# Induced attention in front of two MLPs: narrowing steps placed apart, one softmax for the first chunk, its second block spread early, and second-MLP products held back at exponentials

## The chip, the cores and the metric

The kernel runs on one core of one Trainium2 chip. The metric is the device time of one execution in microseconds, the median of several runs. The core's engines are TensorE (PE in the rows, its weight loads PEld), VectorE (DVE), ScalarE (ACT), GpSimd (POOL) and SyncE (SP), which issues most of the DMAs. Each engine works through its own queue in program order and waits on semaphores for the others.

## What is computed

```python
def mab(q, kv):                       # attention with one head
    s = scale * (q @ kv.transpose(0, 2, 1))
    s = s - s.max(-1, keepdims=True)
    a = np.exp(s)
    a /= a.sum(-1, keepdims=True) + 1e-09
    return a @ kv

h = mab(I, x)            # 32 inducing points over x: 12480 tokens of 128
y = mab(x, h)            # every token over the 32 points
t = y @ w_in;  y = (t * np.cos(t)) @ w_out        # first MLP, 128 -> 2048 -> 128
t = y @ w_in2; y = (t / (1 + np.exp(-t))) @ w_out2  # second MLP, the same sizes
```

The four weight matrices arrive as 64-bit floats.

## The kernel before

The kernel has a prologue, a branch on a flag, and a main loop that is written out in full.

**Heads.** The prologue walks over x in eight heads of 5 to 16 tiles of 128 tokens (`heads`, L70). For each, TensorE transposes the tiles in two halves (`transposes`), ScalarE and VectorE copy them out (`untile`: the first half by ScalarE, the second by VectorE for two groups of 32 rows and then by ScalarE for the other two), TensorE makes the scores against the inducing points, VectorE takes the maximum (`scores`), a running bias is built (`row_max`, `bias`), ScalarE takes the exponential (`exps`), VectorE transposes it (`turn`), and TensorE adds to the attention sum (`induced`, `rescale`). The loop from L565 interleaves these for heads i, i-1 and i-2, and the order of the calls is the order in each engine's queue.

**Narrowing.** A weight matrix is cut into four pieces of 128 x 512; 16 pieces stand in `order` (the first MLP's in and out, then the second's). `fetch` loads a raw 64-bit piece over SP's queue into one of RAW buffers. `narrow_words` makes two parts on ScalarE (body and tail, L137 and L138), `narrow_sign` masks the sign on VectorE (L143), `narrow_join` shifts and joins on VectorE (L148) and adds on POOL (L158), and the next piece is fetched. `begin` runs the ScalarE half and returns the rest as a function to be called later. Pieces 0 to 3 go beside heads 3 to 6, with sign and join behind `turn`; piece 4 in the prologue's end; pieces 5 to 15 in steps 0 to 16 of the main loop, ScalarE's and VectorE's halves in the same step. `split` makes the pair of a rounded value (ScalarE, L172) and the rest (POOL, L173) of a piece.

**Second attention.** Tokens are taken in seven chunks: 8 tiles, five times 16, and 10. For a chunk, `weigh_scores` (TensorE), take, centre, exp, norm, turn and split make the weights: into `s2`, then into `at` and `ahi`, tiles which all chunks share. The chunk's blocks of up to 512 columns are then spread by `spread`: four DMAs of each group of 32 rows, at most 64 KB each, two from `ahi` and two from `at`, into one of two halves of `stk`. Block 0 and block 1 are the first chunk's first and second four tiles in all four groups, so these take 16 DMAs each, or for block 0 a matrix product with `pick` in the prologue; chunk k > 0 has four blocks, one for each group, with four DMAs. In the prologue the first chunk's two halves are two softmaxes (`soft[0]`, `soft[1]`); the second is finished in main steps 1 to 3, and its spread stands at step 4.

**Main loop.** There are 26 blocks of 8 units (a unit is 256 of the 2048 hidden columns), and step s of the loop at L963 runs unit s of the first MLP and unit s - 11 of the second: `mlp1_in` (2 products of TensorE, L752), `mlp2_in` (6, L859), `mlp1_act` (cosine on ScalarE, L781, product on VectorE, L784, rounded half, L790), `mlp2_act` (Silu and rounded half on ScalarE, rest on POOL), `mlp2_out` (unit s - 13), `mlp1_rest` (VectorE, L801) and `mlp1_out` (unit s - 1), the down projections by six products each (L811). In the first 12 units of the first MLP and the first 8 of the second the down projection takes one fp32 product in place of three of the faster form (L821). The hidden values of the second MLP have one PSUM buffer (`h2`), those of the first two. A chunk's take also writes to `h2`. Cosine and Silu need another activation table than the exponential, so each chunk's exponential stands between two table loads on ScalarE. The loop's calls are again the order of the queues:

```python
v = s - L2
if 0 <= v < NU:
    mlp2_in(v)
...
attend(s, True)          # a chunk's exponential
if 0 <= v < NU:
    mlp2_act(v)
```

Of the kernel before, what the change touches and what calls it, by code (L numbers as in the profile page):

```python
# [21 lines left out]
def tile_induced_attention_then_two_mlps(  # L22
# [82 lines left out]
    EARLY = 5  # L105
    PF = 4
    PC, RAW = PF * P, 3
    NP = NF // PF
    raw = persist.tile([P, RAW, PC], I64, name="raw")
    cv = ctx.enter_context(tc.tile_pool(name="cv", bufs=1, reuse_waits="tile"))  # L110
# [18 lines left out]
    parts = {}  # L129

    def narrow_words(name, j):
        words = raw[:, order.index((name, j)) % RAW, :]
        words = words.bitcast(I32).rearrange("p (n w) -> p n w", w=2)
        low, high = words[:, :, 0], words[:, :, 1]
        body = cv.tile([P, PC], F32, tag="body", name="body")
        tail = cv.tile([P, PC], I32, tag="tail", name="tail", bufs=2)
        nc.scalar.mul(body, high.bitcast(F32), 2.0**-112)  # L137
        nc.scalar.mul(tail, low.bitcast(U32), 2.0**-29)  # L138
        parts[name, j] = high, body, tail

    def narrow_sign(name, j):
        sign = cv.tile([P, PC], I32, tag="sign", name="sign")
        nc.vector.tensor_scalar(sign, parts[name, j][0], -(2**31), None, ALU.bitwise_and)  # L143
        parts[name, j] += (sign,)

    def narrow_join(name, j, dst=None):
        high, body, tail, sign = parts.pop((name, j))
        nc.vector.scalar_tensor_tensor(  # L148
            out=sign,
            in0=body.bitcast(I32),  # L150
            scalar=3,
            in1=sign,
            op0=ALU.logical_shift_left,
            op1=ALU.bitwise_or,
        )
        if dst is None:
            dst = tail.bitcast(F32)
        nc.gpsimd.tensor_tensor(dst.bitcast(I32), sign, tail, ALU.add)  # L158
        return dst
# [4 lines left out]
    def split(name, j, v, hi_on=nc.scalar.copy, lo_on=nc.gpsimd):  # L164
        pair = pair_of[name]
        if name[0] == "i":
            hi, lo = (w[:, j * PC : (j + 1) * PC] for w in pair)
        else:
            hi, lo = (
                w[:, PF * j : PF * (j + 1), :].rearrange("p f d -> p (f d)") for w in pair  # L170
            )
        hi_on(hi, v)  # L172
        lo_on.tensor_tensor(lo, v, hi.bitcast(F32), ALU.subtract)  # L173

    narrowed = {}

    def narrow(name, j):

        narrow_words(name, j)
        yield  # L180
        narrow_sign(name, j)
        if name == "in1":
            v = narrow_join(name, j, win[:, j * PC : (j + 1) * PC])
        elif name[0] == "o":
            v = whole_view(name, j)
            narrow_join(name, j, v)
        else:
            v = narrow_join(name, j)
        narrowed[name, j] = v
        fetch()  # L190

    def whole_view(name, j):
        if name in whole_of:
            return whole_of[name][:, PF * j : PF * (j + 1), :].rearrange("p f d -> p (f d)")

    def begin(k):
        step = narrow(*order[k])
        next(step)
        return lambda: next(step, None)
# [26 lines left out]
    def weigh_view(t0, nt, a=0):  # L226
# [4 lines left out]
        for name in ("at", "hi"):  # L231
            st[name] = sft[name][:, a * Q : (a + nt) * Q]
        return st
# [56 lines left out]
    def spread(b, st):  # L290
        t0 = st["span"][0]
        stack = stk[:, b % 2, :]
        for g, t, m, at, n in places(b):
            a = (t - t0) * Q
            for r in range(G):
                src = st["hi"].bitcast(F32) if r < 2 else st["at"]
# [6 lines left out]
    with ExitStack() as pro:  # L303
        pp = pro.enter_context(tc.tile_pool(name="pp", bufs=1))
        pw = pro.enter_context(tc.tile_pool(name="pw", bufs=2))
        ps_s = pro.enter_context(tc.tile_pool(name="ps_s", bufs=2, space=PSUM))
        ps_t = pro.enter_context(tc.tile_pool(name="ps_t", bufs=2, space=PSUM))
        ps_h = pro.enter_context(tc.tile_pool(name="ps_h", bufs=1, space=PSUM))
        ps_m = pro.enter_context(tc.tile_pool(name="ps_m", bufs=1, space=PSUM))
# [25 lines left out]
        for k in range(NH):  # L335
            load(k)
            if 3 <= k < 3 + RAW:
                fetch()
# [223 lines left out]
        end = NH - 1  # L562

        beside = {3: 0, 4: 1, 5: 2, 6: 3}
        for i in range(end):  # L565
            finish = None
# [5 lines left out]
            untile(i, 1)  # L572
            if i >= 2:
                induced(i - 2)
# [14 lines left out]
        untile(end, 0)  # L589
        transposes(end, 1)  # L590
# [5 lines left out]
        scores(end)  # L596
        induced(end - 2, (KT // 2, KT))
# [5 lines left out]
        finish = begin(4)  # L603
# [32 lines left out]
        nc.scalar.activation(sq[:, 0:M], misc[:C, 0:M], AF.Square)  # L636

# [34 lines left out]
        weigh_take(soft[0])  # L672
        weigh_centre(soft[0], nc.vector)
        weigh_exp(soft[0])
        weigh_take(soft[1])
        weigh_centre(soft[1], nc.gpsimd)
        project_hi(0)
        weigh_exp(soft[1])
# [353 lines left out]
```

## Time and profile before

| what | value |
|---|---|
| median of 3 runs | 1006.03 us (1004.76 to 1008.72) |
| the profiled execution | 1005.34 us |
| its span, first to last instruction | 1003.50 us |
| TensorE busy | 968.4 us, 96% |
| VectorE, ScalarE, POOL busy | 788.3, 703.3, 509.0 us |
| heads and first attention, until about | 43 us |
| first product of block 0 | 49.99 us |

A row of a timeline has its start, its length, engine, line, operation, the tiles it writes and reads, and, in brackets, how long the engine stood idle before it and what ended that. TensorE works nearly without a gap from about 120 us on; in front of that the engines take turns in waiting. The granted clock of TensorE is given as a share of full speed, 2.4 GHz; 0.50 is its other level, 1.2 GHz.

### The profile page before, as it was taken

How to read it: one execution, taken by the hardware profiler on the slowest of the kernel's cores; microseconds unless marked ns; L12 is line 12 of the kernel's file. 1: busy time of each engine (PE TensorE's matmuls, PEld its weight loads, DVE VectorE, ACT ScalarE, POOL GpSimd, SP SyncE). 2: the span in 40 equal slices, each digit the busy share in tenths (PEclk: the TensorE clock that was granted, in tenths of full speed). 3: DMA queues.
4: the chain of work that ended last, by engine and by line, in shares of the span. 5: the costliest groups of instructions: out<-in, count | busy, mean ns of one | idle time of the engine just before them, and what ended most of it. 6: DMA issues, size and time to landing. Idle time of an engine off the chain costs nothing.

```text
span 1003.5 us, 12438 instructions
## 1 busy us (share of the span) xinstructions
PE 968.4 (96%) x4667; PEld 774.1 (77%) x4667; DVE 788.3 (79%) x824; ACT 703.3 (70%) x766; POOL 509.0 (51%) x268
## 2 busy tenths in 40 slices
PE   8877999999999999999999999999999999999997
PEld 6533677788887788887788887788887788889996
DVE  4783878898888888888888888888888888867871
ACT  5666566777676777676777676777676777777774
POOL 1143354555554555555565555564545555556555
PEclk9987999999999999999999999999999999999999
DMA  9232000100100100100100100100100100000000
GB/s 339 65 115 85 22 9 14 22 11 10 22 11 11 22 11 12 21 11 11 22 11 11 21 11 11 22 11 11 22 11 11 22 11 8 18 17 11 14 8 16
DMA packets 65230, 28.22 MB, mean 28 GB/s; under 512 B 54312, under 2 KB 59784, under 8 KB 65160
## 3 DMA queue, kind: packets, MB, share of 16 engines
q1 hardware_dynamic: 64504, 27.24, 11.1%
q8 instruction: 39, 0.64, 0.3%
q14 instruction: 31, 0.25, 0.1%
q10 hardware_dynamic: 656, 0.09, 0.1%
HBM read 14.79 MB, written 6.39 MB: 21 GB/s over the span
## 4 chain that ended last, share of the span: by engine, by line
PE 87%; DVE 5%; ACT 4%; issue 2%; SPq 1%; POOL 1%; DMA 0%; DVEq 0%; ACTq 0%; POOLq 0%
PE acc L811 48%; PE h L859 26%; PE h L752 8%; PE acc L821 2%; ACT c L781 2%; PE s L421 1%; SPq L297 1%; ACT L874 1%; ACT s L874 1%; DVE sign L148 1%; DVE h L784 1%; PE pt L388 1%; DVE hi L790 1%; DVE lo L801 1%; DMA stk<-at 0%
## 5 line engine op out<-in xcount | busy, mean ns | idle before, releaser
L883 POOL TENSOR_TENSOR lo<-s,hi 128x1024 fp32r<-128x1024 f32 (+2 forms) x197 | 447.7, 2273 | 390.3 <-ACT hi L882 353.0
L811 PE MATMUL acc<-hi,wo 128*128 128x512 f32 (+2 forms) x1584 | 409.3, 380 | 0.0
L781 ACT ACTIVATE c<-h,half_pi 128x1024 f32<-128x1024 f32 (+2 forms) x208 | 221.0, 1063 | 172.3 <-PE h L752 172.3
L784 DVE TENSOR_TENSOR h<-h,c 128x1024 f32<-128x1024 f32 (+2 forms) x196 | 227.5, 1161 | 140.9 <-ACT c L781 140.6
L811 PEld LDWEIGHTS acc<-hi,wo 128*128 128x128 f32 x1584 | 288.5, 188 | 57.8 <-issue 2.2
L859 PE MATMUL h<-yhi,wi 128*128 128x512 f32 (+2 forms) x832 | 249.1, 381 | 11.7 <-ACT s L874 9.4
L874 ACT ACTIVATE s<-h 128x1024 f32<-128x1024 f32 (+2 forms) x208 | 202.4, 973 | 67.8 <-PE h L859 65.5
L811 PE MATMUL acc<-lo,wo 128*128 128x512 f32 (+2 forms) x792 | 235.4, 378 | 0.1
L790 DVE CAST hi<-h 128x1024 fp32r<-128x1024 f32 (+2 forms) x196 | 226.1, 1153 | 6.8
L801 DVE TENSOR_TENSOR lo<-h,hi 128x1024 fp32r<-128x1024 f32 (+2 forms) x196 | 225.1, 1148 | 5.9
L882 ACT CAST hi<-s 128x1024 fp32r<-128x1024 f32 (+2 forms) x197 | 196.7, 998 | 6.3
L859 PEld LDWEIGHTS h<-yhi,wi 128*128 128x128 f32 x832 | 151.8, 188 | 46.5 <-ACT s L874 14.2
L811 PEld LDWEIGHTS acc<-lo,wo 128*128 128x128 f32 x792 | 145.7, 188 | 29.5 <-POOL lo L888 0.4
L859 PE MATMUL h<-ylo,wi 128*128 128x512 f32 (+2 forms) x416 | 157.4, 378 | 0.0
L752 PE MATMUL h<-stk,hw 128*128 128x512 f32 (+2 forms) x416 | 129.3, 392 | 10.4 <-DMA stk<-at 6.4
L752 PEld LDWEIGHTS h<-stk,hw 128*128 128x128 f32 x416 | 76.8, 191 | 37.3 <-issue 15.0
L859 PEld LDWEIGHTS h<-ylo,wi 128*128 128x128 f32 x416 | 78.4, 188 | 14.6
L844 ACT CAST yhi<-acc 128x512 fp32r<-128x512 f32 (+2 forms) x26 | 14.6, 561 | 18.7 <-PE acc L811 13.7
L821 PE MATMUL acc<-c,wf 128*128 128x512 f32 x48 | 26.7, 685 | 0.9 <-DVE ylo L845 0.9
L845 DVE TENSOR_TENSOR ylo<-acc,yhi 128x512 fp32r<-128x512 f32 (+2 forms) x26 | 16.8, 648 | 8.8 <-ACT yhi L844 8.8
L906 DVE STREAM_TRANSPOSE o<-acc 128x512 f32<-128x512 f32 (+2 forms) x26 | 17.5, 673 | 7.6 <-PE acc L811 7.6
L784 DVE TENSOR_TENSOR c<-h,c 128x1024 f32<-128x1024 f32 x12 | 14.6, 1213 | 9.0 <-ACT c L781 9.0
(141 smaller groups left out, 333.2 us busy)
## 6 DMA issues: line engine op xcount, KB each, us to landing
out_dram<-o SPq DMA_DIRECT2D x80, 64.0 KB, 2.0
x_sb<-in_x_dram SPq DMA_DIRECT2D x8, 512.0 KB, 7.5
raw<-in_moe_w_in_dram SPq DMA_DIRECT2D x8, 512.0 KB, 5.1
raw<-in_moe_w_out_dram SPq DMA_DIRECT2D x8, 512.0 KB, 3.8
stk<-ahi SPq DMA_DIRECT2D x40, 64.0 KB, 2.0
stk<-at SPq DMA_DIRECT2D x40, 64.0 KB, 2.0
x_sb<-in_x_dram SPq DMA_DIRECT2D x3, 256.0 KB, 3.2
x_sb<-in_x_dram SPq DMA_DIRECT2D x2, 320.0 KB, 10.9
```

The source lines that it names most:

```text
L752: nc.tensor.matmul(ps[:, a, 0:n], lhsT=hw[f // 4][:, f % 4 * P : (f % 4 + 1) * P], rhs=stacks[b][:, 0:n], start=True, stop=True,)
L781: nc.scalar.activation(cs, h, AF.Sin, bias=half_pi, scale=1.0)
L784: nc.vector.tensor_tensor(cs if whole else h, h, cs, ALU.mult)
L790: nc.vector.tensor_copy(hi[:, :, 0:n], h)
L801: nc.vector.tensor_tensor(lo[:, :, 0:n], h, hi[:, :, 0:n].bitcast(F32), ALU.subtract)
L811: nc.tensor.matmul(acc[:, 0:n], lhsT=wt[:, 2 * j + a, :], rhs=gt[:, a, 0:n], start=(j == 0 and p == 0 and a == 0), stop=(j == NJ - 1 and p ...
L821: nc.tensor.matmul(acc[:, 0:n], lhsT=w[:, 2 * j + a, :], rhs=c[:, a, 0:n], start=(j == 0 and a == 0), stop=(j == NJ - 1 and a == 1),)
L859: nc.tensor.matmul(ps[:, a, 0:n], lhsT=wt[:, fs], rhs=yt[:, 0:n], start=(p == 0), stop=(p == 2),)
L874: nc.scalar.activation(sv, hid2.pop(u)[:, :, 0:n], AF.Silu)
L882: nc.scalar.copy(hv, sv)
L883: nc.gpsimd.tensor_tensor(lv, sv, hv.bitcast(F32), ALU.subtract)
L906: nc.vector.transpose(o.rearrange("p t d -> p (t d)")[:, 0:n], acc2.pop(b)[:, 0:n])
```

## The change

- **Narrowing in single steps.** `narrow_body`, `narrow_tail`, `narrow_sign` and `narrow_join` are called one by one; body, tail and sign become persistent tiles (two buffers of body and tail), the raw pieces get four buffers instead of three, and the first raw load stands one head earlier in SP's queue. In the heads body goes behind the copies and tail behind the exponentials of heads 2 to 5; sign and join go in front of the scores of heads 3 to 6. Piece 4 is narrowed at the last head and joined behind the projection's start; body and tail of piece 5 go where piece 4 was. In the main loop a piece's join is mostly one step behind its body and tail.
- **One softmax for the first chunk.** The two halves are weighed as one chunk of 8 tiles in the prologue; the steps 1 to 3 of `second` fall away.
- **Block 1 spread in the prologue**, right behind block 0's stack, with the 16 DMAs on SP's queue ahead of the branch; the source of its rest part is `lo0`, a tile of the prologue's pool.
- **Chunk 1's softmax** has its exponential at step 12 instead of 11, norm 13, turn 14 and split in the same step (14.5) instead of the step behind turn.
- **Held back.** In the step behind a chunk's exponential `mlp2_in` and `mlp2_act` stand at the step's end, in the one after it behind `mlp2_out`.
- **Smaller ones.** The cosine's tile has one buffer instead of two from unit 12 on; the prologue's PSUM pools are opened in another order, so the main loop's PSUM tiles take the banks of other tiles; blocks 3 to 5 are spread five steps ahead instead of eight (steps 19, 27 and 35). Chunk 2's turn and split, which write the same `at` and `ahi`, stay at steps 34 and 35, so block 5's spread comes behind them in the order of the program, and copies what chunk 2 left there.

```diff
-        beside = {3: 0, 4: 1, 5: 2, 6: 3}
         for i in range(end):
+            k = i - 2 if i < 2 + NP else None
             ...
             untile(i, 1)
+            if k is not None and k >= 0:
+                narrow_body(k)
             ...
                 exps(i - 1)
-            if i in beside:
-                finish = begin(beside[i])
+            if k is not None and k >= 0:
+                narrow_tail(k)
             if i >= 2:
                 rescale(i - 2)
+            if 0 <= i - 3 < NP:
+                narrow_sign(i - 3)
+                narrow_join(i - 3)
             scores(i)
             if i >= 1:
                 turn(i - 1)
-            if finish:
-                finish()
...
-        soft = [weigh_view(MT * b, MT, MT * b) for b in range(2)]
-        for b, st in enumerate(soft):
-            ps = ps_s.tile([P, W], F32, tag="s1", name="s2")
-            weigh_scores(st, ps[:, 0 : MT * Q])
+        first = chunk_soft[0]
+        weigh_scores(first, ps_s.tile([P, W], F32, tag="s1", name="s2")[:, 0:WF])
...
         stacks[0] = stk[:, 0, :]
+        spread(1, first | {"lo": lo0.bitcast(F32)})
...
-    narrowing = dict(zip((0, 1, 2, 3, 5, 7, 9, 11, 12, 14, 16), order[EARLY:]))
+    worded = dict(zip((0, 1, 2, 4, 6, 8, 10, 12, 14, 16), range(NP + 2, 4 * NP)))
+    joined = dict(zip((0, 1, 2, 3, 5, 7, 9, 11, 13, 15, 17), range(NP + 1, 4 * NP)))
...
-    second = {1: "norm", 2: "turn", 3: "split"}
-    third = {3: "take", 5: "centre", 11: "exp", 12: "norm", 13: "turn", 14: "split"}
+    second = {3: "take", 5: "centre", 12: "exp", 13: "norm", 14: "turn", 14.5: "split"}
...
+                bufs=2 if whole else 1,
...
+        held_back = {}
+        for k in range(1, NK):
+            for s in range(NU):
+                if chunk_step(k, s) == "exp":
+                    held_back[s + 1], held_back[s + 2] = 2, 1
...
+            place = held_back.get(s, 0)
+            into = [False] * 3
             if 0 <= v < NU:
+                into[place] = True
+            if into[0]:
                 mlp2_in(v)
             ...
             attend(s, True)
-            if 0 <= v < NU:
+            if into[0]:
                 mlp2_act(v)
             v = s - L2 - D2
             if 0 <= v < NU:
                 mlp2_out(v)
                 ...
+            v = s - L2
+            if into[1]:
+                mlp2_in(v)
+                mlp2_act(v)
             if s < NU:
                 mlp1_rest(s)
             if s >= L2:
                 out1(s)
+            if into[2]:
+                mlp2_in(v)
+                mlp2_act(v)
```

## Rows read from the trace of the kernel before

**Rows 1.** Page, busy time, share of the span and instructions by engine.

```profile
PE 968.4 (96%) x4667; PEld 774.1 (77%) x4667; DVE 788.3 (79%) x824; ACT 703.3 (70%) x766; POOL 509.0 (51%) x268
```

**Rows 2.** Windows: length, busy of PE, PEld, DVE, ACT, POOL, granted clock, DMA.

```profile
76.40:82.50 6.10, 6.07 (x9) 3.17 (x10) 1.22 (x1) 1.62 (x2) 1.52 (x2) 0.50 0.51 169
...
96.60:100.00 3.40, 3.40 (x8) 2.55 (x9) 1.90 (x2) 3.04 (x5) 1.29 (x1) 0.55 0.02 5
```

**Rows 3.** Timeline of PE, the first transposes of heads 3, 4 and 5.

```profile
15.06 1.09 PE L388 MATMUL pt<-ident,x_sb 128*128 128x128 f32 x8
...
19.52 1.09 PE L388 MATMUL pt<-ident,x_sb 128*128 128x128 f32 x8
...
24.62 1.09 PE L388 MATMUL pt<-ident,x_sb 128*128 128x128 f32 x8
```

**Rows 4.** Timeline of DVE, sign and join of piece 0, the scores' maximum.

```profile
20.96 0.42 DVE L143 TENSOR_SCALAR sign<-raw 128x512 int32<-128x512 int32 x1
21.48 0.69 DVE L148 SCALAR_TENSOR_TENSOR sign<-body,sign 128x512 int32<-128x512 int32 x1
...
24.74 0.69 DVE L431 TENSOR_REDUCE mx<-s 128x1 f32<-128x512 f32 x1 [1.45 <-PE s L421]
```

**Rows 5.** Timeline of DVE, two transposes and the projections' second halves.

```profile
11.38 0.43 DVE L504 STREAM_TRANSPOSE et<-e 128x256 f32<-128x256 f32 x1
...
43.60 0.32 DVE L239 STREAM_TRANSPOSE s<-s 128x128 f32<-128x128 f32 x1 [0.63 <-PE s L218]
...
48.51 2.72 DVE L653 SCALAR_TENSOR_TENSOR hw<-hw,s_w,hwps 128x512 fp32r<-128x512 f32 x4 [0.99 <-ACT hw L650]
```

**Rows 6.** The branch's line (last number: start), and block 0's first product.

```profile
L990 PEldq TENSOR_LOAD <-flag x1: 487/487/487, 47.6 to 47.6; - x1
...
L990 SPq TENSOR_LOAD <-flag x1: 484/484/484, 52.1 to 52.1; - x1
...
49.99 0.74 PE L752 MATMUL h<-stk,hw 128*128 128x512 f32 x2 [1.42 <-ACT stk L698]
```

**Rows 7.** Timeline of PE, main loop: waits and starts of steps.

```profile
76.43 1.19 PE L752 MATMUL h<-stk,hw 128*128 128x512 f32 x2 [5.28 <-DMA stk<-at]
...
90.40 1.03 PE L752 MATMUL h<-stk,hw 128*128 128x512 f32 x2
96.56 1.22 PE L859 MATMUL h<-yhi,wi 128*128 128x512 f32 x2 [5.13 <-ACT s L874]
...
119.04 0.70 PE L752 MATMUL h<-stk,hw 128*128 128x512 f32 x2 [1.11 <-DMA stk<-at]
...
182.58 0.62 PE L752 MATMUL h<-stk,hw 128*128 128x512 f32 x2
...
187.17 0.62 PE L752 MATMUL h<-stk,hw 128*128 128x512 f32 x2
188.68 0.73 PE L859 MATMUL h<-yhi,wi 128*128 128x512 f32 x2 [0.89 <-ACT s L874]
...
192.94 0.62 PE L752 MATMUL h<-stk,hw 128*128 128x512 f32 x2
```

**Rows 8.** Timeline of SP's queue and of POOL: spreads of block 1, split of chunk 1.

```profile
73.69 1.22 SPq L297 DMA_DIRECT2D stk<-at  x2
...
114.70 1.29 POOL L261 TENSOR_TENSOR at<-at,ahi 128x512 f32<-128x512 f32 x1
```

**Rows 9.** Timeline of ACT, the exponential of chunk 1: table loads, Silu.

```profile
92.25 1.28 ACT L247 ACT_TABLE_LOAD   x1
...
94.19 1.28 ACT L874 ACT_TABLE_LOAD   x1
95.49 1.02 ACT L874 ACTIVATE s<-h 128x1024 f32<-128x1024 f32 x1
```

**Rows 10.** Timeline of DVE, the rest of a unit of the first MLP.

```profile
186.90 1.22 DVE L801 TENSOR_TENSOR lo<-h,hi 128x1024 fp32r<-128x1024 f32 x1
```

**Rows 11.** Waits by pair: total us, times, longest.

```profile
DVE h L784 <- ACT c L781: 140.6, 181, 4.6
```

More of the change, by code (lines that the diff above doesn't have):

```diff
@@ L103, in tile_induced_attention_then_two_mlps @@
     }
-    EARLY = 5
     PF = 4
-    PC, RAW = PF * P, 3
+    PC, RAW = PF * P, 4
     NP = NF // PF
     raw = persist.tile([P, RAW, PC], I64, name="raw")
-    cv = ctx.enter_context(tc.tile_pool(name="cv", bufs=1, reuse_waits="tile"))
+    body = persist.tile([P, 2, PC], F32, name="body")
+    tail = persist.tile([P, 2, PC], I32, name="tail")
+    sign = persist.tile([P, PC], I32, name="sign")
     views = {
@@ L127, in fetch, with words_of, narrow_body, narrow_tail @@
         nc.sync.dma_start(out=dst, in_=views[name](j))
[L129 to L147, printed above, removed]
+    def words_of(k):
+        words = raw[:, k % RAW, :].bitcast(I32).rearrange("p (n w) -> p n w", w=2)
+        return words[:, :, 0], words[:, :, 1]
+    def narrow_body(k):
+        nc.scalar.mul(body[:, k % 2, :], words_of(k)[1].bitcast(F32), 2.0**-112)
+    def narrow_tail(k):
+        nc.scalar.mul(tail[:, k % 2, :], words_of(k)[0].bitcast(U32), 2.0**-29)
+    def narrow_sign(k):
+        nc.vector.tensor_scalar(sign, words_of(k)[1], -(2**31), None, ALU.bitwise_and)
+    def narrow_join(k):
         nc.vector.scalar_tensor_tensor(
             out=sign,
-            in0=body.bitcast(I32),
+            in0=body[:, k % 2, :].bitcast(I32),
             scalar=3,
@@ L155, in narrow_join, with narrowed, split @@
         )
[L156 to L159, printed above, removed]
+        nc.gpsimd.tensor_tensor(
+            narrowed(k).bitcast(I32), sign, tail[:, k % 2, :], ALU.add
+        )
+        fetch()
+    def narrowed(k):
+        name, j = order[k]
+        if name == "in1":
+            return win[:, j * PC : (j + 1) * PC]
+        if name in whole_of:
+            return whole_of[name][:, PF * j : PF * (j + 1), :].rearrange("p f d -> p (f d)")
+        return tail[:, k % 2, :].bitcast(F32)
     pair_of = {"out1": wo1}
     whole_of = {"out1": wf1, "out2": wf2}
-    def split(name, j, v, hi_on=nc.scalar.copy, lo_on=nc.gpsimd):
-        pair = pair_of[name]
+    def split(k):
+        name, j = order[k]
+        v = narrowed(k)
         if name[0] == "i":
-            hi, lo = (w[:, j * PC : (j + 1) * PC] for w in pair)
+            hi, lo = (w[:, j * PC : (j + 1) * PC] for w in pair_of[name])
         else:
             hi, lo = (
-                w[:, PF * j : PF * (j + 1), :].rearrange("p f d -> p (f d)") for w in pair
-            )
[L172 to L199, printed above, removed]
+                w[:, PF * j : PF * (j + 1), :].rearrange("p f d -> p (f d)")
+                for w in pair_of[name]
+            )
+        nc.scalar.copy(hi, v)
+        nc.gpsimd.tensor_tensor(lo, v, hi.bitcast(F32), ALU.subtract)
     def width(span, g):
@@ L765, in mlp1_act @@
             whole = u < WHOLE1
-            c = u1.tile([P, 2, W], F32, tag=("hi1", "lo1")[u % 2] if whole else "c", name="c")
+            c = u1.tile(
+                [P, 2, W],
+                F32,
+                tag=("hi1", "lo1")[u % 2] if whole else "c",
+                name="c",
+                bufs=2 if whole else 1,
+            )
             cs = c[:, :, 0:n]
@@ L948, in soften, with chunk_step @@
                 weigh_split(st, nc.scalar.copy, nc.gpsimd)
+        def chunk_step(k, s):
+            if k == 1:
+                return second.get(s)
+            return later.get(s + LEAD - first_of[k] * NJ)
         def attend(s, early):
-            todo = [(soft[1], second.get(s)), (chunk_soft[1], third.get(s))]
-            for k in range(2, NK):
-                todo.append((chunk_soft[k], later.get(s + LEAD - first_of[k] * NJ)))
-            for st, what in todo:
-                if what and (what == "exp") == early:
-                    soften(st, what)
-        def fill(s):
-            for b in range(1, NB):
-                if s == (4 if b == 1 else b * NJ - (1 if b == 2 else FILL)):
-                    spread(b, chunk_soft[blocks[b][0]] if b > 1 else soft[1])
+            for k in range(1, NK):
+                for at in (s, s + 0.5):
+                    what = chunk_step(k, at)
+                    if what and (what == "exp") == early:
+                        soften(chunk_soft[k], what)
+        def fill(s):
+            for b in range(2, NB):
+                if s == b * NJ - (1 if b == 2 else 5 if blocks[b][0] == 1 else FILL):
+                    spread(b, chunk_soft[blocks[b][0]])
+        held_back = {}
+        for k in range(1, NK):
+            for s in range(NU):
+                if chunk_step(k, s) == "exp":
+                    held_back[s + 1], held_back[s + 2] = 2, 1
         for s in range(NU + L2 + D2 + 1):
```

56 lines of the change are left out of this document (31 added, 25 removed).

## The prediction

> **What bounds the kernel now.** I read the page's busy table first, then the windows by stage, then TensorE's own timeline for every idle stretch. TensorE is busy 96% of the span [rows 1], and from 145.8 us on the idle rows on it are few, so the main loop can't be shortened by moving work; only idle time can go, and time at the lower clock. The windows show where that lies [rows 2]: 6.1 us at a granted clock of 0.50 from 76.4 on, and 3.4 us at 0.55 from 96.6 on. In front of each TensorE stood idle [rows 7]: 5.28 us for the transfers that fill the stack of block 1, 5.13 us for the Silu of the second MLP. Then 1.11 us for block 2's stack, and 0.89 us for a Silu at 188.68, a row that comes back at each of the five later exponentials. In the heads (until 43 us) the chain runs through VectorE.
>
> **Heads.** A head without narrowing in front takes 19.52 - 15.06 = 4.46 us, one behind it 24.62 - 19.52 = 5.10 [rows 3]. VectorE does sign and join (0.42 and 0.69) straight after turn, and the next head's half copy, for which ScalarE's half and then the scores wait, is queued behind; later the same engine waits 1.45 us for the scores [rows 4]. The change puts sign and join into that gap. 1.1 fits in 1.45 as long as the gap stays; with the earlier scores it shrinks, and max and turn then start some 0.35 late, which the next transposes cover. Two heads gain 0.6 each, the third 0.3 (11 tiles), the last about 0.5: 1.9 us, ends 0 and 2.6. body and tail go one head earlier, body ahead of the exponential: 0.6 us in ScalarE's queue, hidden because turn stands behind the max (0.6 a head if it didn't). The raw loads go one head earlier on SP's queue, ahead of x loads; no wait of TensorE in the heads is for a load, and they would have to slip by a head (4.46) to show: nothing.
>
> **One softmax of 8 tiles.** Nine passes of 256 columns instead of 128. A transpose is 0.43 at 256 against 0.32 [rows 5]; 0.11 to 0.15 each is 1.2 us. VectorE stood idle 0.99 us before the projections' second halves, waiting for ScalarE [rows 5], and no longer does the second block's passes in between: left over 0.25 (0 to 0.6). The join of piece 4 goes into the 0.63 us gap in front of the transpose [rows 5]: 0.1. So the prologue yields 1.9 - 0.35 = about 1.6 (0 to 2.4).
>
> **Block 1's spread early.** Its 16 DMAs take 1.22 per two on SP's queue [rows 8], so 10 us; started when the first softmax's split is there (about 48) they end at 58 and land before 61, ten microseconds ahead of step 8. Behind them on SP stand its flag load and the next raw load (needed at step 4, about 63): 0 to 1.2 us of ScalarE, which I carry below. lo0 is now read until 60; by the tile sizes it lies 69 KB into the prologue's pool, where the main loop (63 to 72 KB) has wi2, first written in step 4: nothing. So the 5.28 goes, and with it the 6.1 us at half clock, worth 3.0. Its norm, turn and split also leave steps 1 to 3.
>
> **Steps 8 to 12.** Without the wait step 8 starts at 76.43 - 5.28 = 71.2. Before, steps 8 to 12 took 90.4 - 76.4 = 14.0 [rows 7], less 3.0 for the clock is 11; I followed join on POOL, split on ScalarE, then cosine (still in that order) and take 11.8: step 12 at 83.0. Step 11 has no exponential now, so the 5.13 wait goes too.
>
> **Steps 12 to 16, what is late next.** The exponential stands in step 12, and ScalarE reaches its table load 4.25 us into it (estimates from the 1.02 of a Silu [rows 9]: the first Silu and a split hold it 2.0 us beyond the step's start, cosine 1.1, body and tail 1.15): 87.25. From there to the first product of block 2: load, exponential and load back 95.49 - 92.25 = 3.24 [rows 9]; Silu and a split 1.6, cosine 1.1; on VectorE six passes of 1.22 [rows 10] for units 13 and 14 (7.3), sign and join 1.1 [rows 4], norm 1.6 (est.: a 512 column reduce and three small steps), turn 0.7 (est. from [rows 5]); the split on ScalarE 0.6; from the POOL half of the split to TensorE 119.04 - 114.70 = 4.34 [rows 7, 8]. Sum 21.6, so step 16 at 108.8 instead of 119.04. TensorE's own work from 83.0: 90 passes of 512 columns in steps 12 to 15 at 4.59/20 = 0.23 [rows 7] are 20.7 (an fp32 product of the whole form counted as four), plus some 0.5 of waiting for the first Silu: it is ready at 104.2. So **a new wait of about 4.6 us** stands at step 16, because turn and split now share a step behind lo of unit 14 (ScalarE waits in order at that split, and the next cosine behind it). The stretch gains 119.0 - 108.8 = 10.2; ends: only the first wait gone, 5.3, and no new wait, 14.8. After 5.28 and 5.13 us of idling the clock was low for 6.1 and 3.4 us, after 1.11 the products run at full pace [rows 2, 7]; for 4.6 I take the middle price, 1.5 us (0 to 3).
>
> **The five later exponentials.** A step is 187.17 - 182.58 = 4.59; the one with the Silu wait 192.94 - 187.17 = 5.77, so 1.18 each [rows 7]. With the second MLP's products last in that step, TensorE first does 12 products of the two down projections, 2.8 us; they need the lo tile of the step before, done at 186.90 + 1.22 = 188.1 [rows 10]. It comes to the held-back products at 190.4, the Silu ends at 188.6. The second step keeps one down projection (1.4 us) in front of its products, so the Silu of the first, 1.8 us late, is in time, and POOL's lo stays ahead of the down projection two steps on. All of it goes: 5 x 1.18 = 5.9 (4 to 5.9).
>
> By the Trainium skill (ScalarE: Activation LUTs, What ACT_TABLE_LOAD costs) a switch of tables is about 1.28 us and a drain of 1.38. The trace shows the load back at 1.28 and Silu 1.30 after its start [rows 9], so no drain. By the skill's sum two switches would take 2.8 more, the Silu would end at 191.4, and 1.0 us of each wait would stay: 5 us less in all.
>
> **Sum.** 1.6 + 10.2 - 1.5 + 5.9 = 16.2. The profiled run took 1005.34 (span 1003.50, 1.84 outside), so 989.1; the median of the runs shown is 0.7 above it, 1006.03. I say **989**. Fills of blocks 3 to 5 three steps later still leave five steps (23 us): nothing. The other PSUM banks free unit 1's scores from the projections' last reader, but unit 2's wait for VectorE as before: nothing.
>
> **Rivals.**
> No new wait at step 16 (VectorE further ahead than my sum): 989 - 4.6 - 1.5 = 983. For it: small passes overlap in their rows. Against: nine things in order between exponential and stack. 0.12.
> The conditional is a meeting point, or the first product waits for the 16 transfers: the main loop starts when SP has issued them, at 58.6 and not at 50.0 [rows 6], 8.6 us later: 997.6. Against: TensorE loaded the flag at 47.6 and began block 0 at 49.99, SP loaded it only at 52.1 [rows 6]. 0.06.
> The hold-back does nothing (its products wait for lo or Silu anyhow) and the heads' gap closes: 989 + 5.9 + 1.6 = 996.5. For it: the gap was measured with late scores. 0.12. This and the one before together: 1004, 0.04.
> **Slower:** c has one buffer instead of two past unit 12. ScalarE's cosine of unit u+1 must then wait for VectorE's product of unit u. If that couples the two by 0.1 us in each of 196 steps, it is +19.6: 1009. It decides from the point where the product of u ends after the scores of u+1 are there. Against: VectorE waits for the cosine in 181 units, 140.6 us in all [rows 11], 0.78 each, so it is through with unit u long before. 0.04.
>
> **Chances.** Forecast 0.62 (own range 985 to 993). A measurement tells about 0.5% (5 us). Faster by more: forecast, no new wait, and each single loss, 0.92; within: both losses, 0.04; slower 0.04. The range goes from no new wait to the hold-back failing: 983 to 997.
>
> **What would show it.** Right: no DMA wait near 70 us and no clock of 0.50 there; no Silu wait in step 12; starts of heads 4.5 apart; a wait for stk of 3 to 5 us at step 16; no 0.89 rows. Wrong: TensorE's first product of block 0 after 55; ScalarE waiting for VectorE's product at the cosine; a Silu row left at the exponentials. The forecast fails first in the length of the chain from exponential to stack.

## The result and the profile after

The changed kernel takes 993.08 us in the median of 4 runs (991.96 to 993.71), beside 1006.22 for the kernel before on the same chip: a ratio of 0.9866, with a 95% interval of 0.9844 to 0.9888. Its profiled execution took 992.66 us, with a span of 990.8. So the time fell by 13.1 us where 17 were forecast, and the span by 12.7 where the sum said 16.2.

The page's busy line, and windows of the stretch from step 8 to step 17 (length, busy of PE, PEld, DVE, ACT, POOL, granted clock, DMA share, GB/s). They answer to [rows 1, 2].

```profile
PE 966.6 (98%) x4659; PEld 773.5 (78%) x4659; DVE 786.5 (79%) x818; ACT 703.1 (71%) x764; POOL 507.9 (51%) x265
```

```profile
69.00:103.00 34.00, 31.95 (x102) 18.52 (x100) 24.47 (x28) 24.36 (x32) 14.95 (x14) 1.00 0.15 43
103.00:107.00 4.00, 0.06 (x1) 0.09 (x1) 3.07 (x4) 2.25 (x3) 1.16 (x1) 0.79 0.28 68
107.00:114.00 7.00, 7.00 (x17) 4.53 (x18) 5.23 (x5) 3.28 (x4) 2.52 (x2) 0.63 0.15 37
```

TensorE loses 4 us once, between 103 and 107, and runs at 0.63 of its clock behind that; the two stretches at 0.50 and 0.55 in [rows 2] are gone. TensorE's timeline shows which wait it is; these rows answer to [rows 6, 7]. L733 is the first product of a step, so its rows are the starts of steps 0, 2, 8, 12 and 16.

```profile
48.83 1.20 PE L733 MATMUL h<-stk,hw 128*128 128x512 f32 x4 [0.74 <-ACT stk L680]
...
53.16 1.22 PE L733 MATMUL h<-stk,hw 128*128 128x512 f32 x2 [3.13 <-DVE c L773]
...
69.50 0.79 PE L733 MATMUL h<-stk,hw 128*128 128x512 f32 x2
...
81.31 1.04 PE L733 MATMUL h<-stk,hw 128*128 128x512 f32 x2
82.89 0.72 PE L853 MATMUL h<-yhi,wi 128*128 128x512 f32 x2 [0.54 <-ACT s L868]
...
106.94 1.19 PE L733 MATMUL h<-stk,hw 128*128 128x512 f32 x2 [4.04 <-DMA stk<-at]
...
154.95 0.74 PE L853 MATMUL h<-yhi,wi 128*128 128x512 f32 x2 [0.42 <-DVE s L220]
...
194.92 1.20 PE L805 MATMUL acc<-hi,wo 128*128 128x512 f32 x4 [0.18 <-DVE ylo L839]
```

The wait for block 1's stack at step 8 (5.28) and the Silu wait behind it (5.13) have gone. A wait of 4.04 for block 2's stack has come, at the place and nearly of the size that the prediction gave. The 3.13 at step 2 is no new loss: without the wait for block 1's stack, steps 0 to 8 take 26.44 - 5.28 = 21.2 us in the kernel before and 20.7 here. The last row is new: TensorE waits for `ylo`, and it stands in step 33, three steps behind the one that had the 0.89 [rows 7].

All kernels of this study can be read in one table. Each number is the distance between two step starts (first products of steps, as above) in TensorE's timeline of the profiled run; the second column is the start of step 0, step 25 is the one behind chunk 2's take, steps 30 and 33 are the first and the fourth of those around its exponential.

| kernel | step 0 | 0 to 8 | 8 to 12 | 12 to 16 | 16 to 17 | 25 | 30 | 33 | 17 to last | 0 to last |
|---|---|---|---|---|---|---|---|---|---|---|
| before | 49.99 | 26.44 | 13.97 | 28.64 | 5.03 | 5.38 | 5.77 | 4.60 | 847.75 | 921.83 |
| changed | 48.83 | 20.67 | 11.81 | 25.63 | 7.51 | 5.41 | 4.60 | 5.04 | 844.54 | 910.16 |
| no hold-back | 49.07 | 20.79 | 11.81 | 25.78 | 5.03 | 5.41 | 5.77 | 4.60 | 847.80 | 911.21 |
| later norm | 47.91 | 20.62 | 11.80 | 25.57 | 6.65 | 5.41 | 4.60 | 4.59 | 842.19 | 906.83 |
| exponential at 11 | 47.76 | 20.62 | 11.82 | 24.82 | 4.98 | 5.38 | 4.60 | 5.03 | 844.41 | 906.65 |
| block 1 late | 48.50 | 25.75 | 12.52 | 25.54 | 7.91 | 5.40 | 4.59 | 5.04 | 844.54 | 916.26 |
| heads as before | 49.80 | 21.01 | 11.81 | 25.54 | 7.77 | 5.40 | 4.59 | 5.04 | 844.51 | 910.64 |
| spread 8 ahead | 49.03 | 20.80 | 11.80 | 25.55 | 7.61 | 5.42 | 4.59 | 5.04 | 844.48 | 910.24 |
| hold at takes | 49.06 | 20.83 | 11.80 | 25.55 | 7.65 | 4.74 | 4.60 | 5.04 | 840.97 | 906.80 |
| four edits | 49.04 | 20.80 | 11.81 | 24.85 | 4.98 | 4.74 | 4.59 | 4.60 | 838.69 | 901.13 |
| exponential at 10 | 48.78 | 20.64 | 12.20 | 26.83 | 4.97 | 4.74 | 4.60 | 4.59 | 838.70 | 903.34 |
| same, no first hold | 48.78 | 20.67 | 11.80 | 27.21 | 4.98 | 4.74 | 4.59 | 4.60 | 838.69 | 903.35 |
| same, Silu's table | 48.33 | 20.62 | 12.21 | 24.24 | 4.98 | 4.74 | 4.60 | 4.59 | 838.69 | 900.74 |
| four edits again | 48.17 | 20.62 | 11.79 | 24.85 | 4.96 | 4.73 | 4.59 | 4.60 | 838.73 | 900.95 |

From before to changed, the columns give -1.2, -5.8, -2.2, -3.0, +2.5 and, from step 17 to the last, -3.2: -12.8 in all.

### The profile page after: what moved, and what is told of

It is laid out like the page before. It is cut to its first block, busy times and chain, and to the rows that moved or that the text cites. A ratio compares the mean times of both kernels' runs of the same rounds, so it can differ in the third digit from the quotient of the medians.

```text
span 990.8 us, 12394 instructions
## 1 busy us (share of the span) xinstructions
PE 966.6 (98%) x4659; PEld 773.5 (78%) x4659; DVE 786.5 (79%) x818; ACT 703.1 (71%) x764; POOL 507.9 (51%) x265
## 4 chain that ended last, share of the span: by engine, by line
PE 80%; DVE 9%; ACT 3%; issue 2%; POOL 1%; DMA 0%; SPq 0%; ACTq 0%; POOLq 0%
PE acc L805 46%; PE h L853 24%; PE h L733 8%; DVE lo L795 2%; DVE h L773 2%; DVE hi L779 2%; ACT c L768 2%; PE acc L815 1%; ACT s L868 1%; DVE ylo L839 1%; POOL tail L152 0%; DVE sm L232 0%; DVE sm L233 0%; DVE s L220 0%; DVE sign L144 0%
## 5 line engine op out<-in xcount | busy, mean ns | idle before, releaser
L733 PE MATMUL h<-stk,hw 128*128 128x512 f32 (+2 forms) x416 | 128.2, 389 | 8.0 <-DMA stk<-at 4.0
L733 PEld LDWEIGHTS h<-stk,hw 128*128 128x128 f32 x416 | 76.4, 190 | 33.7 <-issue 12.1
L815 PE MATMUL acc<-c,wf 128*128 128x512 f32 x48 | 24.3, 632 | 1.4 <-DVE ylo L839 1.4
```

What stands on the lines that cost most here:

```text
L733: nc.tensor.matmul(ps[:, a, 0:n], lhsT=hw[f // 4][:, f % 4 * P : (f % 4 + 1) * P], rhs=stacks[b][:, 0:n], start=True, stop=True,)
L815: nc.tensor.matmul(acc[:, 0:n], lhsT=w[:, 2 * j + a, :], rhs=c[:, a, 0:n], start=(j == 0 and a == 0), stop=(j == NJ - 1 and a == 1),)
```

## The experiments

The changed kernel is the base of the first seven. Ratios are to the kernel before, run beside each on the same chip.

**Without the hold-back.**

```diff
-                    held_back[s + 1], held_back[s + 2] = 2, 1
+                    pass
```

> The changed kernel without the hold-back: the second MLP's products stand at their old place in every step. Theory (the chain from chunk 1's exponential to block 2's stack sets step 16): the wait moves from step 16 to step 13, some 4 us for a Silu, step 16 starts at 106.9 give or take 1 as before, and the five later exponentials lose the 0.65 us each that they gained net, so about 3 to 4 us slower in all; the 0.89 us rows come back and the 0.18 us rows for ylo go. Rival (the hold-back itself removed the first 5 us wait and pays 1.18 at each later one): 9 to 11 us slower, step 16 at 111 or later.

Measured: 994.73 us (993.97 to 996.84), ratio 0.9891 (0.9867 to 0.9915); 1.65 above the changed kernel, not 3 to 4. The intervals of the two ratios overlap, so the columns have to tell them apart. TensorE's idle rows behind the exponential up to step 16, and a window of the same run:

```profile
90.19 0.74 PE L853 MATMUL h<-yhi,wi 128*128 128x512 f32 x2 [3.11 <-ACT s L868]
...
107.45 0.69 PE L733 MATMUL h<-stk,hw 128*128 128x512 f32 x2 [0.86 <-DMA stk<-at]
```

```profile
90.20:114.00 23.80, 22.94 (x81) 15.21 (x82) 19.65 (x21) 13.69 (x18) 8.72 (x7) 1.00 0.09 22
```

Two things cancel. The five later exponentials lose 5.77 - 4.60 = 1.17 each without it and give back the 0.44 at step 33 (844.54 to 847.80, 3.3 in all), so there the hold-back works. At chunk 1's exponential it gains nothing up to step 16, which begins 58.1 us after step 0 with it and 58.4 without. Without it, TensorE idles in two pieces (3.11 and 0.86) and keeps clock 1.00 in this trace; with it nearly all of the idle time is one piece of 4.04, and step 16 takes 7.51 instead of 5.03. That two pieces are what kept the clock isn't shown: this is one execution, and the pair of runs at the end has a shorter idle stretch behind which the clock fell in one of them.

**The later chunks' norm one step later.**

```diff
-    later = {0: "take", 2: "centre", 5: "exp", 7: "norm", 10: "turn", 11: "split"}
+    later = {0: "take", 2: "centre", 5: "exp", 8: "norm", 10: "turn", 11: "split"}
```

> Norm of chunks 2 to 6 one step later (8 instead of 7 behind the take), so that on VectorE it stands behind the ylo of the block that ends in that step. Theory (the give-back of 0.45 us per later chunk, four steps after each exponential, is VectorE's norm standing in front of ylo while VectorE is 1.2 us late): the five rows of TensorE waiting for ylo go, 2.0 to 2.2 us faster. Rival (VectorE is late there because of the late cosine alone): the rows stay, within 0.5 us.

Measured: 989.45 us (988.84 to 990.34), ratio 0.9836 (0.9816 to 0.9857): 3.6 under the changed kernel, more than the 2.0 to 2.2 expected. First VectorE in the changed kernel around the new row at 194.92, then the same place with the norm later:

```profile
189.27 0.67 DVE L232 TENSOR_REDUCE sm<-s 128x16 f32<-128x512 f32 x1
189.97 0.37 DVE L233 TENSOR_SCALAR sm<-sm 128x16 f32<-128x16 f32 x1
...
194.19 0.68 DVE L839 TENSOR_TENSOR ylo<-acc,yhi 128x512 fp32r<-128x512 f32 x1
```

```profile
191.03 0.68 DVE L839 TENSOR_TENSOR ylo<-acc,yhi 128x512 fp32r<-128x512 f32 x1
191.62 0.68 DVE L232 TENSOR_REDUCE sm<-s 128x16 f32<-128x512 f32 x1
```

The norm's three steps (0.67, 0.37 and a reciprocal of 0.25) stood in VectorE's queue ahead of `ylo`, which reads `acc1`, a tile with one buffer; TensorE's next down projection waits for that buffer. With `ylo` ahead of the norm the step of 5.04 is 4.59, five times, and the stretch from 17 on 2.35 shorter; that much is shown to be this edit's. The rest stands in the columns for step 0 (0.9) and 16 to 17 (0.9), in front of the first place that the edit touches; both differ between kernels that share that part (below).

**Chunk 1's exponential at step 11, the rest of its softmax one step earlier.**

```diff
-    second = {3: "take", 5: "centre", 12: "exp", 13: "norm", 14: "turn", 14.5: "split"}
+    second = {3: "take", 5: "centre", 11: "exp", 12: "norm", 13: "turn", 13.5: "split"}
```

> Chunk 1's exponential, norm, turn and split one step earlier (11, 12, 13, 13.5), the hold-back with it (steps 12 and 13). Theory (the chain from exponential to stack sets step 16): the chain starts some 3.5 us earlier and ends some 3 us earlier, step 16 at 104 instead of 106.9; TensorE waits 2 to 3 us in step 12 for the first Silu instead, and its clock stays up: 2.5 to 5 us faster. Rival (step 16 is late because ScalarE waits in order at the split of the same step, wherever the exponential is): step 16 within 1 us of 106.9, total unchanged or up to 3 us slower through the new wait in step 12.

Measured: 988.94 us (988.05 to 989.8), ratio 0.9831 (0.981 to 0.9852). TensorE's only idle row from 80 to 110:

```profile
85.13 0.73 PE L853 MATMUL h<-yhi,wi 128*128 128x512 f32 x2 [2.19 <-ACT s L868]
```

```profile
86.00:90.00 4.00, 4.00 (x10) 2.50 (x9) 3.30 (x3) 4.00 (x6) 1.73 (x2) 0.59 0.02 4
```

The stack's wait goes, a shorter one for Silu comes. Steps 12 to 17 take 29.80 instead of 33.14, and of these 3.34 us 2.53 are the clock behind step 16. That the clock would stay up behind the new wait was wrong: the window shows 0.59. The stretch up to step 16 is 0.8 shorter all the same.

**Block 1 spread in the main loop again.**

```diff
-        spread(1, first | {"lo": lo0.bitcast(F32)})
+            if s == 3:
+                soften(chunk_soft[0], "split")
+            if s == 4:
+                spread(1, chunk_soft[0])
```

> One softmax as in the changed kernel, but block 1's split done again at step 3 and its 16 transfers at step 4, as before the change. Theory (the early transfers are the largest single part): the wait for the stack at step 8 comes back with 4 to 6 us and the half clock behind it with 2.5 to 3: 6 to 9 us slower. Rival (it was the second softmax's work in steps 1 to 3 that made the transfers late): SP starts at 58 instead of 64 and the wait is 0 to 2 us, 0 to 2 us slower.

Measured: 998.1 us (997.92 to 998.58), ratio 0.992 (0.99 to 0.9941): 5.0 us slower, where 6 to 9 were expected; from step 0 on it is 6.1. TensorE's timeline at step 8, and the window behind it:

```profile
74.25 1.19 PE L732 MATMUL h<-stk,hw 128*128 128x512 f32 x2 [5.19 <-DMA stk<-at]
```

```profile
74.20:80.00 5.80, 5.75 (x13) 3.16 (x13) 1.23 (x1) 2.74 (x4) 1.28 (x1) 0.72 0.58 180
```

The old wait is back with its old size, 5.1 us in the column from 0 to 8 and 0.7 in the next; the early spread is what removed it, and not the second softmax that left steps 1 to 3. The clock behind it fell for less time than in the kernel before: 0.72 here, 0.50 in [rows 2].

**Sign and join behind turn again.**

```diff
-            if 0 <= i - 3 < NP:
-                narrow_sign(i - 3)
-                narrow_join(i - 3)
             scores(i)
             if i >= 1:
                 turn(i - 1)
+            if 0 <= i - 3 < NP:
+                narrow_sign(i - 3)
+                narrow_join(i - 3)
```

> The changed kernel with sign and join of heads 3 to 6 put back behind turn; body and tail keep their new places. Measured from the first scores of head 0 to the weighing of the first chunk, the changed kernel took 34.81 us and the kernel before 36.79. Theory (sign and join behind turn are what made a head 5.10 instead of 4.46): this stretch is 36.4 to 36.9 again, the time 2.0 us over the changed kernel's, 995. Rival (the earlier raw loads or body and tail in single steps made the heads shorter): the stretch stays within 0.5 us of 34.8 and the time within 0.5 of 993.

Measured: 995.04 us (993.94 to 995.96), ratio 0.9887 (0.9868 to 0.9907): 1.96 slower. The stretch from the first scores to the weighing takes 43.14 - 6.63 = 36.5 us, 1.7 more than in the changed kernel. VectorE in one head, first the changed kernel, then this one:

```profile
24.37 0.42 DVE L141 TENSOR_SCALAR sign<-raw 128x512 int32<-128x512 int32 x1
24.83 0.69 DVE L144 SCALAR_TENSOR_TENSOR sign<-body,sign 128x512 int32<-128x512 int32 x1
25.44 0.68 DVE L412 TENSOR_REDUCE mx<-s 128x1 f32<-128x512 f32 x1
```

```profile
24.97 0.69 DVE L412 TENSOR_REDUCE mx<-s 128x1 f32<-128x512 f32 x1 [1.41 <-PE s L402]
...
26.30 0.42 DVE L141 TENSOR_SCALAR sign<-raw 128x512 int32<-128x512 int32 x1
```

The gap of 1.41 in front of the maximum is the one of [rows 4]; with sign and join in it, the maximum follows without a gap.

**Blocks 3 to 5 spread eight steps ahead.**

```diff
-                if s == b * NJ - (1 if b == 2 else 5 if blocks[b][0] == 1 else FILL):
+                if s == b * NJ - (1 if b == 2 else FILL):
```

> The changed kernel with blocks 3 to 5 spread eight steps ahead again instead of five (so block 5's spread comes ahead of chunk 2's turn and split in the order of the program, and copies chunk 1's weights, as in the kernel before). Theory: five steps are 23 us, the transfers land in a few, so the place is worth nothing either way: within 0.5 us of 993. Rival (the later spread takes SP's queue or the tile at longer and so delays chunk 2's softmax, or is late for its block): 1 us or more below 993, with another idle row of TensorE at steps 24 to 40 in one of the two.

Measured: 992.97 us (991.25 to 993.59), ratio 0.9859 (0.984 to 0.9878). No distance in the table moves by more than 0.13: the place of these transfers costs nothing. In the changed kernel block 5's spread, at step 35, stands behind chunk 2's turn and split and copies chunk 2's weights for 512 tokens of chunk 1; eight steps ahead it copies the right ones, at no cost in time.

**A hold-back behind the takes.**

```diff
+                if k > 1 and chunk_step(k, s) == "take":
+                    held_back[s + 1] = 1
```

> The changed kernel with one hold-back more: in the step behind each later chunk's take (which writes the scores through h2) the second MLP's products and Silu stand behind its own down projection. In the changed kernel that step has TensorE waiting 0.42 us for VectorE's take, and takes 5.41 us where its neighbours take 4.59. Theory (take and h2 set that step): 0.7 to 0.8 us off in each of five steps, 3.5 to 4 us in all, 989.5. Rival (the wait moves to the Silu's rounded half or to POOL's lo, as the hold-back at the exponentials moved part of its wait to acc1): within 1 us of 993.

Measured: 989.28 us (987.54 to 990.14), ratio 0.9822 (0.9803 to 0.9841). Step 25 takes 4.74 instead of 5.41, and the stretch from 17 on is 3.6 shorter. TensorE's row at 154.95 with 0.42 has no successor in this run, and no other wait took its place.

**Four edits at once:** the exponential at 11, the later norm, eight steps ahead, the hold-back behind the takes.

> The changed kernel with four edits at once: chunk 1's exponential at step 11, norm, turn and split a step earlier too; the later chunks' norm two steps earlier than the turn (8 instead of 7); blocks 3 to 5 spread eight steps ahead; the hold-back behind the takes. Theory (they touch different waits: the stack's wait at step 16, the ylo rows of the exponentials, the take's step): the gains add up, 3.3 + 2.2 + 3.5 = 9 us below the changed kernel, 984. Rival (the exponential at step 11 and the later norm both got their gain out of the same low clock around step 17): 2 us less, 986 to 987. Rival (hold-back at the takes gives nothing): 987.5.

Measured: 984.0 us (982.39 to 984.47), ratio 0.977 (0.9754 to 0.9786), 9.1 under the changed kernel. Steps 12 to 17 give 3.3 and the stretch from 17 on 5.85, which is 2.35 + 3.57 of the single edits to 0.1. They add up, since each takes a wait of its own. Two waits for Silu are left, 2.21 at 86.60 and 1.52 at 101.89; from step 16 on TensorE's timeline has no idle row.

**The exponential one step earlier still,** at step 10, with norm, turn and split at 11, 12 and 12.5, then the same **without the hold-back at chunk 1's exponential:**

```diff
-                if chunk_step(k, s) == "exp":
+                if chunk_step(k, s) == "exp" and k > 1:
```

> The kernel with four edits, with chunk 1's exponential, norm, turn and split one step earlier still (10, 11, 12 and 12.5). At step 11 its TensorE waited 2.21 us at 86.60 and 1.52 us at 101.89 for a Silu, the first in the step behind the exponential, the second two steps behind the split. Theory (ScalarE's two table loads and exponential, 3.2 us, are what the first Silu of the second MLP waits for; at step 10 there is no such Silu yet): the 2.21 goes, the second may stay, 1.5 to 2.2 us off: 982. Rival (ScalarE is behind by as much anyhow, with body, tail, two splits and cosines in its queue): the wait appears one step earlier or later at the same size, within 0.5 us of 984.

> The same kernel, the exponential at step 10, without the hold-back at chunk 1's exponential; the five later hold-backs stay. Theory (as in the kernel without any hold-back, at the first exponential it only moves a wait): within 0.7 us of the run with it. Rival (with the exponential in front of the second MLP's first products it finds nothing to fill and only delays them): 1 to 2 us less.

Measured: 985.87 (984.03 to 986.54), ratio 0.9774 (0.9745 to 0.9803), and 986.16 (982.53 to 986.81), ratio 0.9771 (0.9738 to 0.9804). By the columns 2.2 us longer than the four edits from step 0 on, all of it before step 16; hold-back or not makes no difference there. ScalarE around the exponential at step 10, TensorE's wait and the window behind it:

```profile
78.64 1.28 ACT L228 ACT_TABLE_LOAD   x1
...
81.09 1.28 ACT L768 ACT_TABLE_LOAD   x1
...
83.52 1.28 ACT L868 ACT_TABLE_LOAD   x1
84.81 1.02 ACT L868 ACTIVATE s<-h 128x1024 f32<-128x1024 f32 x1
```

```profile
85.89 1.22 PE L853 MATMUL h<-yhi,wi 128*128 128x512 f32 x2 [3.64 <-ACT s L868]
```

```profile
85.90:91.20 5.30, 5.30 (x10) 3.17 (x11) 5.16 (x7) 4.14 (x6) 4.28 (x4) 0.50 0.01 3
```

The wait didn't go, as theory had it, and didn't keep its size, as the rival had it: it grew. With the cosine next behind the exponential, the table that is loaded for it doesn't serve the Silu, and a third load stands in front of the first Silu. The kernel before and the changed one have Silu next, and load twice [rows 9].

**The exponential at step 10, with a small Silu behind it.**

```diff
                 weigh_exp(st)
+                if st is chunk_soft[1]:
+                    nc.scalar.activation(st["m2"], st["m2"], AF.Silu)
```

> The exponential at step 10 as before, and behind it on ScalarE one Silu of a small tile that nobody reads (the maxima of chunk 1, already used), so that the table that is loaded back serves Silu and cosine. With the exponential at step 10 alone the profile had three loads, at 78.64 for the exponential, 81.09 for a cosine and 83.52 for the first Silu; with it at step 11 two. Theory (the third load, 1.28 us, stands in front of the first Silu, for which TensorE waited 3.64 us at 85.89 and then ran at half clock): the wait is 2.3 to 2.4 us, no half clock behind it, and from the first step's start to step 16 it takes 55.7 us instead of 59.7 (57.5 with the exponential at step 11): 982 to 982.5. Rival (the wait is for ScalarE's queue as a whole, and the clock falls after the idle time all the same): 59.7 less 1.3, no faster than the run beside it with the exponential at step 11.

Beside it on the same chip the four edits again:

> The kernel with four edits once more, unchanged, on the same chip as the run with the table for Silu, so that the two can be compared: 984 where the kernel before has 1006.2; two loads of tables at the exponential, waits of 2.2 and 1.5 us for Silu at steps 12 and 15, 57.5 us from the first step's start to step 16.

Measured: 983.24 us (980.73 to 983.38), ratio 0.9747 (0.9728 to 0.9766), beside 982.91 (982.61 to 984.4), ratio 0.9758 (0.974 to 0.9775). ScalarE, TensorE and a window of the run with the small Silu:

```profile
80.11 1.28 ACT L938 ACT_TABLE_LOAD   x1
81.40 0.22 ACT L938 ACTIVATE m<-m 128x16 f32<-128x16 f32 x1
...
82.03 1.11 ACT L768 ACTIVATE c<-h,half_pi 128x1024 f32<-128x1024 f32 x1
83.04 1.01 ACT L868 ACTIVATE s<-h 128x1024 f32<-128x1024 f32 x1
```

```profile
84.11 1.22 PE L853 MATMUL h<-yhi,wi 128*128 128x512 f32 x2 [2.32 <-ACT s L868]
```

```profile
84.10:88.00 3.90, 3.90 (x9) 2.75 (x10) 3.80 (x7) 3.56 (x6) 2.40 (x2) 0.59 0.02 4
```

The table was the cause: one load less, and the wait is 2.32 as expected. That the clock would stay up was wrong: it was 0.59 behind the wait, and from step 0 to 16 it takes 57.1 us, not 55.7; the four edits take 57.3. In the clock, and in being no faster than the run beside it, the rival was right. The two are level, and both beat the changed kernel by about 10 us.

The four edits, one program, were profiled twice. The idle stretch in step 12 is 2.21 us in one execution and 2.19 in the other. A window behind it and the second wait in the first of them, then the same window in the other:

```profile
87.00:91.00 4.00, 4.00 (x16) 2.55 (x15) 2.82 (x3) 4.00 (x7) 1.61 (x2) 1.00 0.01 4
```

```profile
101.89 0.73 PE L853 MATMUL h<-yhi,wi 128*128 128x512 f32 x2 [1.52 <-ACT s L868]
```

```profile
87.00:91.00 4.00, 4.00 (x8) 1.99 (x7) 3.90 (x4) 3.54 (x5) 1.62 (x2) 0.58 0.00 0
```

Behind the same idle time the clock stayed at 1.00 once and fell once. Where it fell, the second wait of 1.5 us, which was expected again, is missing, and steps 12 to 16 take 24.85 in both: the slow stretch of TensorE took the place of a wait for ScalarE and cost nothing.

## Why the prediction was right, and where its sum was off

The forecast of 989 lies 4 us under the measured 993, which is inside the range of 983 to 997, but at the upper end of the 985 to 993 that it gave to the forecast alone; the direction and the places were right. Its sum was 3.5 us too large against the profiled span, by these steps.

**Heads: right.** From the first scores to the weighing, the changed kernel takes 42.16 - 7.35 = 34.8 us, the kernel before 43.12 - 6.33 = 36.8: 2.0 gained, 1.9 forecast. TensorE's first transposes and the first and the last row of that stretch, of the kernel before and then of the changed one:

```profile
4.63 1.09 PE L388 MATMUL pt<-ident,x_sb 128*128 128x128 f32 x8
6.33 0.94 PE L421 MATMUL s<-xF,indT 128*32 128x256 f32 x8 [0.61 <-DVE xF L403]
...
43.12 0.65 PE L218 MATMUL s<-xF,hT 128*32 128x128 f32 x16
```

```profile
5.01 1.73 PE L369 MATMUL pt<-ident,x_sb 128*128 128x128 f32 x8
7.35 0.94 PE L402 MATMUL s<-xF,indT 128*32 128x256 f32 x8 [0.61 <-DVE xF L384]
...
42.16 0.64 PE L198 MATMUL s<-xF,hT 128*32 128x256 f32 x8
```

With sign and join put back 1.7 of the 2.0 is lost, so that step is shown; the last 0.3 isn't assigned. The first transposes of heads 3 to 6 start at 16.08, 20.54, 25.18 and 29.73 in the changed kernel, 4.5 apart as forecast [rows 3]. The later start, 1.0 us, can't be put down to the change: in the changed kernel and the runs built on it, whose program is the same up to there, the same product starts between 6.29 and 7.58. The rows show where it lies: the eight first transposes begin 0.4 later and take 0.6 longer. It is in the span and not in the sum.

**One softmax of 8 tiles: sign wrong, small.** From the weighing to step 0 it is 48.83 - 42.16 = 6.67 instead of 49.99 - 43.12 = 6.87, 0.2 less where 0.35 more was forecast. No run takes this step alone.

**Block 1's spread, steps 0 to 12: right.** SP's queue, the first and the last of the eight rows:

```profile
46.94 1.25 SPq L278 DMA_DIRECT2D stk<-ahi  x2
...
55.84 1.22 SPq L278 DMA_DIRECT2D stk<-lo  x2
```

They end at 57.1 (58 forecast), and TensorE began block 0 at 48.83 while SP was still issuing. That refutes the rival of the conditional as a meeting point. From step 0 to 12 the gain is 7.9 (5.8 + 2.2 in the columns), and putting the spread back costs 5.0 in the whole time.

**Steps 12 to 16: right in each term.** The timelines of ScalarE, VectorE and POOL along the chain:

```profile
85.50 1.28 ACT L228 ACT_TABLE_LOAD   x1
...
87.45 1.28 ACT L868 ACT_TABLE_LOAD   x1
88.74 1.02 ACT L868 ACTIVATE s<-h 128x1024 f32<-128x1024 f32 x1
...
102.20 0.62 ACT L241 CAST ahi<-at 128x512 fp32r<-128x512 f32 x1 [4.62 <-DVE at L238]
```

```profile
91.32 1.23 DVE L773 TENSOR_TENSOR h<-h,c 128x1024 f32<-128x1024 f32 x1 [3.18 <-ACT c L768]
...
101.46 0.70 DVE L238 STREAM_TRANSPOSE at<-s 128x512 f32<-128x512 f32 x1
```

```profile
102.89 1.26 POOL L242 TENSOR_TENSOR at<-at,ahi 128x512 f32<-128x512 f32 x1 [3.86 <-ACT ahi L241]
```

The load stands 4.2 us into step 12 (4.25 forecast), from there to block 2's first product it is 106.94 - 85.50 = 21.4 (21.6), and TensorE's own work up to the wait 106.94 - 4.04 - 81.31 = 21.6 (21.2). So the wait is 4.04 and not 4.6. VectorE's part is the long one: from the product behind the cosine, at 91.32, to the end of turn, at 102.16, it works without a gap, and ScalarE stood idle 4.62 us for turn. A Silu wait of 0.54 stands in step 12; the sum had it, at 0.5, and the list of signs, which wants none, had not.

**The clock behind the wait: mis-sized.** Step 16 takes 7.51 where the step after takes 4.98, so 2.5 us; the middle price taken was 1.5, with 3 as the upper end. Part of this is chance: six kernels of the table have this wait, at 3.96 to 4.04 us, and their step 16 takes 6.65 to 7.91, a price of about 1.6 to 2.9. The run without the hold-back shows none at all in its trace: 3.11 and 0.86 us of idle time, and a clock of 1.00.

**The later exponentials: the term that failed.** The sentence "All of it goes: 5 x 1.18 = 5.9 (4 to 5.9)" followed h2, the lo tile and POOL. It didn't follow `acc1`. The 0.89 rows are gone, as forecast, and step 30 takes 4.60; but the idle time had let VectorE catch up, and with TensorE on time `ylo` is late behind norm: 0.44 is given back at step 33 and at its like behind the four later ones, and 0.3 in all in the steps behind these. Measured 3.2, under the lower end of the term. The run with the later norm shows the cause. The table loads are as in [rows 9]: two of 1.28, and Silu at 88.74, 1.29 behind the start of the second. The Trainium skill (ScalarE: Activation LUTs, What ACT_TABLE_LOAD costs) would have a drain of 1.38 at each, and this trace has none.

**The rivals.** No new wait at step 16: refuted by the 4.04. The hold-back that does nothing: refuted at the later exponentials, and true at the first, which the prediction didn't set apart. The slower case, ScalarE waiting for VectorE through the single buffer of `c`: the view of waits by pair has no row for ScalarE's cosine waiting for the product, and the pair of [rows 11] stays near what it was:

```profile
DVE h L773 <- ACT c L768: 136.2, 173, 3.2
```

A kernel with two buffers wasn't run, but from step 17 on no step differs by more than 0.04 us between the two kernels except where the later exponentials stand, so the one buffer costs nothing that shows there. For both losses together the prediction says 1004, where its own terms (8.6 and 7.5) give 1005.

In terms of the sum: the later start +1.0, later exponentials +2.7, clock +1.0; the softmax -0.55 and the stretch up to step 16 -0.7. Together +3.45 of the 3.5. Of these the first, 1.0, and about as much of the clock differ between executions of the same code, so some 2 us of the miss may be chance; the term that was wrong in its mechanism is the later exponentials.

## What to carry to other kernels

When a wait is taken away, list every buffer with one copy on the loop's cycle and ask who will be late for it now: the engine that used the idle time to catch up is the next one, and a small softmax step in its queue was enough here (0.44 us, five times). Look for the same edit's other places: the hold-back that paid 1.17 at each exponential paid 0.67 at each take, a place the change left alone. An idle stretch of TensorE can be dearer than its length, since the clock may fall behind it: here 4.0 us cost 2.5 more. One trace doesn't tell that price: behind 2.2 us the same program kept its clock once and lost it once. In that pair the lost clock cost nothing, since a longer chain on the other engines set the next step: it took the place of a wait.

## What the runs showed of the chip

- The price of an idle stretch in clock isn't fixed by its length. The clock fell behind 5.19, 4.04, 3.64, 2.32 and, in two traces, 2.19 us (means of 0.72, 0.63, 0.50, 0.59, 0.59 and 0.58 over the windows of 4 to 7 us above); behind 3.11 and, with the same program as one of the 2.19, behind 2.21 it stayed at 1.00. What tells these apart stays open.
- A load that stood in front of a cosine, behind the exponential, brought a table without Silu, and 1.28 us more for a third load, although a table with both exists (81.40 to 83.04 above, with no load). The Trainium skill (ScalarE activation tables: per-element evaluation and per-set limits, Table sets in the compiler and the runtime) says that in each block loads are placed for the longest run of functions that one set serves; if cosine and Silu stand in one block here, the third load at 83.52 doesn't agree with that.
- The same first eight transposes took 1.09 to 1.97 us and began at 4.59 to 5.01 from run to run (first scores at 6.29 to 7.58). The sum had no term for it, and the cause stays open.
